# Chunked attention followed by a gated feed-forward layer: crossbar transposes, block-diagonal attention matmuls, and per-token division

## The chip, the cores and the metric

The kernel runs on 1 core of one Trainium2 chip. The metric is device time in microseconds (us), the median over repeated executions. The profile's span is a little shorter than that time: one profiled run of 405.57 us has a span of 403.8 us.

A core has a matmul engine (PE), a vector engine (DVE), an activation engine (ACT), a general engine (POOL) and SP, which in these kernels does nothing but issue DMAs. In this kernel each engine gets one list of instructions and works through it in order.

## The reference

```python
# q, k, v: [batch 8, heads 8, seq 576, dim 64]; chunks of 64 tokens, no attention across chunks
scores = q_c @ k_c.transpose(...) / 8          # 64 x 64 per (batch, head, chunk)
attn   = exp(scores - max); attn /= attn.sum(-1) + 1e-9
out    = attn @ v_c
x      = out as [4608 tokens, 512]
h      = x @ w_in                               # 512 -> 2048
g      = h * (1 / (1 + exp(-beta * h)))
return g @ w_out                                # 2048 -> 512, float32
```

Both kernels work in 9 blocks of 512 tokens, with bfloat16 matmuls. The two dense layers, mm1 (`x @ w_in`) and mm2 (`g @ w_out`), take 1,152 matmuls of 128x512. Four of them start every 0.864 us in the trace, so they need 1152 / 4 x 0.864 = 248.8 us at full clock, or 27.65 us per block. Everything above that is what a rewrite can win.

## The kernel before

A small scheduler collects calls with `at(time, function, ...)`, sorts them by that made-up time (16 units to a block in this kernel), and so fixes the order of every engine's list. Times are only an order. The parts that matter, with cuts marked `...`:

```python
def transpose_dma(blk):                 # q and k of a block, 32 tiles of 128x128, one DMA
    P.dma("sp", lambda e: e.dma_start_transpose(qkT[...], qkcast[...]), ...)

def scores(blk, hp):                    # 64 matmuls of 64x64x64 per block
    ...
    e.matmul(A[64*g:64*g+64, ...], kT[r, 2*cc+g, :], qT[r, 2*cc+g, :])

def sums(blk, bank):                    # softmax denominators: 16 matmuls against a matrix of ones
def invert(blk, bank):                  # DVE: reciprocal, Rhi, Rs
def spread(blk, u, banks):              # 16 matmuls carry the reciprocals to all the rows
    ...
    e.matmul(A[:, banks[g], col:col+128], sel[:, u, ...], Rs[:, :])
def normalize(blk, u, g, bank):         # DVE: o * reciprocal, written straight into xT
    ...

def mm2(blk, s, part, bank):
    ...
    if part == 3:                       # result copied by ACT, stored by ACT's own DMA queue
        P.dma("act", lambda e: e.dma_start(out[n0:n0+128, :], ostage[...]), ...)

for blk in range(3, NB):
    ...
    loads = 30.5 if blk == 3 else t0 - 24
    for which in range(2):
        at(loads, load_qk, blk, which)
    at(loads + 0.1, load_v, blk)
    ...
    at(41 if blk == 3 else t0 - 15.5, transpose_dma, blk)
    attention(blk, t0, u)
```

SP carries loads and one transpose per block. The attention result x is produced already transposed by the matmuls, and the stores are on ACT's queue.

The softmax here doesn't subtract the row's maximum and nothing guards it: scores larger than these inputs give would overflow.

## Time and profile before

| | before |
|---|---|
| time, median of 3 runs | 345.63 us (344.17 to 346.78) |
| span of the profile | 342.4 us |
| needed by mm1 and mm2 at full clock | 248.8 us |
| period of a steady block (start of scores to start of scores) | 32.6 us |
| first mm1 | 24.5 us |

From the page of the kernel before, parts 1, 2 and 4 (busy time of each engine; the span in 40 slices, busy share in tenths; the engines' shares of the chain of work that ended last, where SPq is SP's queue):

```profile
PE 298.1 (87%) x2645; PEld 147.6 (43%) x2688; DVE 150.3 (44%) x234; ACT 167.6 (49%) x264; POOL 112.6 (33%) x124
PE   1559978886598969989998999999999999999996
PEclk9999999999879989999999999999999999999999
DMA  7988997988999889889982990450000000110012
PE 69%; ACT 7%; DVE 7%; DMA 7%; SPq 5%; issue 3%; POOL 1%; ACTq 0%; POOLq 0%
```

PE is the bound: it is busy nearly everywhere after the start, and 69% of the last chain is PE.

From the timeline of PE in the kernel before (start us, duration us, engine, line, operation, output and inputs, shapes, number; in brackets the idle time just before and what ended it): one scores group, one AV group (the attention weights times v), and most of one spread.

```profile
137.45 1.51 PE L383 MATMUL A<-qkO 64*64 64x64 bf16 x64
145.04 0.48 PE L430 MATMUL A<-E,v_bf 64*64 64x64 bf16 x32
130.05 0.56 PE L417 MATMUL A<-Rs,sel 128*128 128x128 bf16 x7 [0.47 <-DVE xT L442]
```

From the timeline of SP in the kernel before, one whole steady period. A duration on SP is the time SP spends issuing, not the transfer.

```profile
185.43 5.72 SPq L341 DMA_TRANSPOSE qkT<-qkcast  x1
191.20 1.24 SPq L268 DMA_DIRECT2D qkstage<-in_q_dram  x2
192.48 1.25 SPq L268 DMA_DIRECT2D qkstage<-in_k_dram  x2
193.77 8.43 SPq L280 DMA_DIRECT2D vstage<-in_v_dram  x4
218.02 5.85 SPq L341 DMA_TRANSPOSE qkT<-qkcast  x1
```

SP works for 16.6 us of the 32.6 and is then free for 16 us.

### The profile page before, as it was taken

How to read it: one execution, taken by the hardware profiler on the slowest of the kernel's cores; microseconds unless marked ns; L12 is line 12 of the kernel's file. 1: busy time of each engine (PE TensorE's matmuls, PEld its weight loads, DVE VectorE, ACT ScalarE, POOL GpSimd, SP SyncE). 2: the span in 40 equal slices, each digit the busy share in tenths (PEclk: the TensorE clock that was granted, in tenths of full speed). 3: DMA queues.
4: the chain of work that ended last, by engine and by line, in shares of the span. 5: the costliest groups of instructions: out<-in, count | busy, mean ns of one | idle time of the engine just before them, and what ended most of it. 6: DMA issues, size and time to landing. Idle time of an engine off the chain costs nothing.

```text
span 342.4 us, 6271 instructions
## 1 busy us (share of the span) xinstructions
PE 298.1 (87%) x2645; PEld 147.6 (43%) x2688; DVE 150.3 (44%) x234; ACT 167.6 (49%) x264; POOL 112.6 (33%) x124
## 2 busy tenths in 40 slices
PE   1559978886598969989998999999999999999996
PEld 0433335443334434534454454445444444444442
DVE  3354712484443455255534543463356336443300
ACT  1545725476234625464455546554655565544421
POOL 0366602334187582690096019403800000000000
PEclk9999999999879989999999999999999999999999
DMA  7988997988999889889982990450000000110012
GB/s 244 292 325 305 300 237 203 222 233 189 188 221 184 211 182 218 227 227 207 240 181 49 267 270 33 93 93 33 31 33 31 33 33 31 47 48 31 31 65 90
DMA packets 79116, 52.85 MB, mean 154 GB/s; under 512 B 65776, under 2 KB 65776, under 8 KB 79088
## 3 DMA queue, kind: packets, MB, share of 16 engines
q1 hardware_dynamic: 71840, 43.00, 52.2%
q10 hardware_dynamic: 7248, 9.45, 8.2%
q8 instruction: 21, 0.34, 0.4%
q14 instruction: 7, 0.06, 0.0%
HBM read 36.71 MB, written 9.44 MB: 135 GB/s over the span
## 4 chain that ended last, share of the span: by engine, by line
PE 69%; ACT 7%; DVE 7%; DMA 7%; SPq 5%; issue 3%; POOL 1%; ACTq 0%; POOLq 0%
PE F L469 30%; PE F L453 30%; DMA qkstage<-in_k_dram 5%; ACT tt L459 3%; SPq L268 3%; PE A L383 3%; PE A L417 3%; DVE R L403 2%; DVE g L462 2%; PE A L430 2%; SPq L341 2%; DMA qkstage<-in_q_dram 2%; DVE Rs L407 1%; ACT E L390 1%; PE A L396 1%
## 5 line engine op out<-in xcount | busy, mean ns | idle before, releaser
L462 DVE SCALAR_TENSOR_TENSOR g<-tt,F 128x512 bf16<-128x512 bf16 x144 | 99.0, 687 | 145.5 <-ACT tt L459 145.4
L459 ACT ACTIVATE tt<-F,beta_half 128x512 bf16<-128x512 f32 x144 | 98.9, 687 | 117.2 <-PE F L453 117.1
L453 PE MATMUL F<-xT,w_in_bf 128*128 128x512 bf16 x549 | 146.0, 391 | 4.3 <-issue 1.8
L469 PE MATMUL F<-w_out_bf,g 128*128 128x512 bf16 x560 | 140.8, 379 | 2.2 <-issue 1.1
L453 PEld LDWEIGHTS F<-xT,w_in_bf 128*128 128x128 bf16 x576 | 55.5, 100 | 68.4 <-issue 6.1
L469 PEld LDWEIGHTS F<-w_out_bf,g 128*128 128x128 bf16 x576 | 54.9, 98 | 64.6 <-DVE g L462 1.1
L330 POOL COPY qkO<-qkT 128x1024 bf16<-128x1024 bf16 x24 | 45.9, 1954 | 75.0 <-PE A L383 55.0
L330 POOL CAST qkcast<-qkstage 128x1024 bf16<-128x1024 f32 x28 | 28.2, 1041 | 23.6 <-DMA qkstage<-in_k_dram 9.9
L474 ACT ACTIVATE ostage<-F 128x512 f32<-128x512 f32 x36 | 21.5, 597 | 25.7 <-PE F L469 25.7
L330 POOL CAST v_bf<-vstage 128x512 bf16<-128x512 f32 x36 | 21.0, 615 | 23.9 <-DMA vstage<-in_v_dram 23.9
L442 DVE TENSOR_TENSOR xT<-o_sb,A 128x512 bf16<-128x512 f32 x36 | 24.1, 681 | 3.3 <-ACT o_sb L437 2.2
L417 PE MATMUL A<-Rs,sel 128*128 128x128 bf16 x144 | 12.9, 239 | 14.5 <-DVE Rs L407 10.9
L437 ACT ACTIVATE o_sb<-A 128x512 f32<-128x512 f32 x32 | 18.8, 593 | 10.3 <-ACT ostage L474 4.6
L390 ACT ACTIVATE E<-A 128x512 bf16<-128x512 f32 x36 | 20.7, 594 | 5.9 <-PE A L383 3.8
L417 PEld LDWEIGHTS A<-Rs,sel 128*128 128x128 bf16 x144 | 10.0, 107 | 21.0 <-DVE Rs L407 15.0
L383 PE MATMUL A<-qkO 64*64 64x64 bf16 x576 | 12.7, 196 | 4.7 <-DVE qkO L330 2.8
L383 PEld LDWEIGHTS A<-qkO 64*64 64x64 bf16 x576 | 11.5, 110 | 8.3 <-issue 3.6
L403 DVE RECIPROCAL R<-A 128x128 f32<-128x128 f32 x9 | 8.6, 952 | 11.3 <-PE F L430 6.1
L357 PE MATMUL F<-identity,qkcast 128*128 128x128 bf16 x32 | 4.1, 311 | 9.3 <-DVE qkcast L330 7.9
L322 POOL CAST w_out_bf<-wstage 128x512 bf16<-128x512 f32 x16 | 9.1, 613 | 5.5 <-DMA wstage<-in_moe_w_out_dram 5.5
L310 POOL CAST w_in_bf<-wstage 128x512 bf16<-128x512 f32 x14 | 8.3, 630 | 5.4 <-DMA wstage<-in_moe_w_in_dram 5.2
L430 PEld LDWEIGHTS A<-E,v_bf 64*64 64x64 bf16 x512 | 5.8, 111 | 7.4 <-issue 3.6
(32 smaller groups left out, 66.5 us busy)
## 6 DMA issues: line engine op xcount, KB each, us to landing
out_dram<-ostage ACTq DMA_DIRECT2D x36, 256.0 KB, 2.6
vstage<-in_v_dram SPq DMA_DIRECT2D x32, 256.0 KB, 8.8
wstage<-in_moe_w_in_dram SPq DMA_DIRECT2D x4, 1024.0 KB, 9.8
wstage<-in_moe_w_out_dram SPq DMA_DIRECT2D x4, 1024.0 KB, 9.6
qkstage<-in_q_dram SPq DMA_DIRECT2D x4, 512.0 KB, 4.1
qkstage<-in_k_dram SPq DMA_DIRECT2D x4, 512.0 KB
qkstage<-in_q_dram SPq DMA_DIRECT2D x4, 448.0 KB
qkstage<-in_k_dram SPq DMA_DIRECT2D x4, 448.0 KB
```

The costliest lines, as they stand in the source:

```text
L330: P.op(eng, lambda e: e.tensor_copy(dst, src), reads, writes)
L383: return e.matmul(A[64 * g:64 * g + 64, 2 * u + hb, col:col + 64], kT[r, 2 * cc + g, :], qT[r, 2 * cc + g, :])
L390: P.op("act", lambda e: e.activation(E[:, bank, :], A[:, bank, :], AF.Exp, scale=0.125), reads=[K("A", bank, v=("s", blk))], writes=[K("E" ...
L403: P.op("dve", lambda e: e.reciprocal(R[:, :], A[:, bank, 0:128]), reads=[K("A", bank, v=("l", blk))], writes=[K("R", v=blk)])
L417: return e.matmul(A[:, banks[g], col:col + 128], sel[:, u, 2 * (2 * w + ch) + g, :], Rs[:, :])
L437: P.op("act", lambda e: e.activation(o_sb[:, g, :], ps[:, bank, :], AF.Copy), reads=[K(psname, bank, v=("o", blk, u))], writes=[K("o_sb", ...
L442: P.op("dve", lambda e: e.tensor_tensor(xT[:, sx, 2 * u:2 * u + 2, :].rearrange("p w (c g i) -> p w c g i", c=4, g=2)[:, :, :, g, :], o_sb ...
L453: P.op("pe", lambda e, c=c: e.matmul(F[:, bank, :], w_in_bf[:, c, 128 * t:128 * t + 128], xT[:, sx, c, :], start=(c == 0), stop=(c == NC - ...
L459: P.op("act", lambda e: e.activation(tt[:, T % 3, :], F[:, bank, :], AF.Tanh, scale=beta_half[:, t:t + 1]), reads=[K("F", bank, v=("h", T) ...
L462: P.op("dve", lambda e: e.scalar_tensor_tensor(g2[:, sg, t, :], tt[:, T % 3, :], 1.0, F[:, bank, :], ALU.add, ALU.mult), reads=[K("F", ban ...
L469: P.op("pe", lambda e, t=t: e.matmul(F[:, bank, :], g2[:, sg, t, 128 * s:128 * s + 128], w_out_bf[:, t, :], start=(t == 0), stop=(t == NT ...
L474: P.op("act", lambda e: e.activation(ostage[:, N % NOS, :], F[:, bank, :], AF.Copy, scale=0.5), reads=[K("F", bank, v=("o", N))], writes=[ ...
```

## The change

The intent is to take attention work off PE. Scores and AV become full 128-row matmuls: k is widened into block-diagonal 128x128 tiles (two heads at once), so a block needs 32 score matmuls instead of 64. v gets a column of ones, so AV yields the softmax denominator as its 65th column. Then `sums` and `spread` disappear, and DVE divides per token. The price is that x now comes out with tokens on rows and must be transposed, which is given to the DMA crossbar. The first two blocks are worked by halves so that mm1 can begin sooner. The diff, 931 lines, cut to its core:

```diff
+        def scores(h, u, n, tiled=False):            # h is half a block: 256 tokens
+            ...
+                kk = kO[...] if tiled else kBD[:, s, hp, c, :]
+                e.matmul(..., kk, q_of(h, r, c, hp))  # q: every 4th element of qkT
+        def attend(h, u, banks, tiled=False):
+            ...
+                e.matmul(unit_out(banks[hp2], c, 65, r), EBD[:, s, u, i, :],
+                         v_bf[r, sv, 2 * u + hp2, 4 * hv + c, 0:65])
-        def sums(...) / invert(...) / spread(...)
+        def normalize(h, u, banks):
+            P.op("dve", lambda e: e.reciprocal(R[:, u, :, :], o[:, :, :, 64]), ...)
+            P.op("dve", lambda e: e.tensor_tensor(xn[...], o[:, :, :, 0:64], R[...], ALU.mult), ...)
+        def turn_x_dma(h):                           # 16 tiles of 128x128, twice per block
+            P.dma("sp", lambda e: e.dma_start_transpose(xT[...], xn[...]), ...)
-            P.dma("act", ... out[n0:n0 + 128, :] ...)
+        def store(blk, s, n, cols=(0, 512), eng="act", queues=("sp", "sp")):
+            ...                                      # two DMAs of 64 rows
+        def load_qk(h, which, queue):
+            ...                # last block, which gathers from 8 batches: 4 DMAs for each of the others' one
+        for blk in range(3, NB):
+            b = begin(blk)                           # 90 + 29.5 * (blk - 3)
+            for h in (2 * blk, 2 * blk + 1):
+                for which in range(2):
+                    at(b - 34, load_qk, h, which, "sp")
+            for hb in range(2):
+                at(b - 33.5, load_v, blk, hb, (0, 1), "sp")
+            rest(2 * blk, b - 27, b - 24.5, b - 20.5, b - 15, 1.74, b - 9.5, b - 17)
+            rest(2 * blk + 1, b - 24, b - 21.5, b - 15.5, b - 10, 1.74, b - 4.5, b - 12)
```

`rest(h, tc, tx, tk, t0, step, tX, tv)` places the cast of q and k at `tc`, their transpose at `tx`, the widening of k at `tk`, scores to division from `t0` on, the transpose of x at `tX` and the cast of v at `tv`.

## The prediction

> **What bounds it now.** TensorE. The page's part 1 has PE 87% busy; the expert layer alone is 1,152 matmuls of 128x512, and in the timeline four of them start every 0.864 us, so they need 248.8 us at full clock. Span 342.4 us: 94 us are lost to them:
> 1. Start. The first mm1 begins at 24.5 us (timeline).
> 2. Until about 105 us. The busy windows show some 235 of the 1,152 matmuls done by then, so about 54 us were lost (start included). The chain of waits gives: loads of k to 84.0, cast, DMA transpose (5.60 us to issue), loads to 104.0, reordering on POOL (1.95 us each).
> 3. Steady blocks. The reciprocal recurs every 32.6 us (185.6, 218.2, 250.8), against 27.65 us for 128 matmuls: 4.9 us of attention per block. Timeline: 64 scores matmuls 1.44 us, AV 2x0.5, sums 0.4, spread 2x0.5, the rest drains around tiled forms and waits for Rs, xT.
>
> **What the change does to PE.** Sums and spread go (the ones column gives the sum, DVE divides per token). Scores become 32 and AV 32 matmuls per block, 128 stationary columns and 64/65 moving. The spread matmuls (128x128, new weights each) run at 57 ns; half the columns should cost 28 to 57. I take 35 ns, 2.2 us per block (estimate; the Trainium skill, "TensorE: Matmul & The Clock Gate", Back-to-back issue gap, puts the floor near 25 ns). No tiling switch remains in steady blocks. Steady block: 32.6 to about 30 us, 6 times, saving 16 us.
>
> **Early part.** The first half block needs half the q, k, v, and no reciprocal, Rhi, Rs, spread chain. First mm1 near 17 to 18 us, not 24.5. Block 1 by halves fills the gap 41 to 75. Loads run in the windows at 385 GB/s for weights and q/k, about 225 for v (256-byte rows). Weights (21.5 us), four blocks of q, k, v (41 us), block 2's transposes and stores (13 us): block 3's q and k are in near 70 us, against 104 now. Lost PE time to the steady state: about 25 us instead of 54.
>
> **Other engines, off PE's path.** Per block: POOL about 15 us, ACT 18, DVE 15. DMA is tight: transposes go from 32 tiles of 128x128 per block to 48. The six now take about 7.5 us of all 16 engines each (busy windows 218 to 226), for 1 MB that loads in 2.7. The Trainium skill ("Advanced Engine Details and Errata", X-Bar Transpose) has transposes as fast as regular DMAs; this trace doesn't agree. Estimate per block: q, k 5.5, v 4.7, transposes 11.2, store 3: 24.4 of 30 us. SP issues all of it, near 25 us per block, stores behind loads.
>
> **Sum.** 248.8 + 25 (start and early) + 7 x 2.2 + 3 (tail) + 3 (median over span) = 295 us. Range 284 to 308. Chances: faster by over 2% 0.97, same 0.02, slower 0.01.
>
> **What shows it.** Busy windows: first mm1 by 18 us; period of the scores 29.5 to 30.5 us, POOL, ACT, DVE below 65%. Timeline: 16 score or AV matmuls in 0.4 to 0.9 us with no idle before them. PEclk 1.0 after 20 us; DMA over 80% busy until the last loads.
>
> **What would make it wrong.** SP or the DMA engines saturate: PE idles before scores or mm1 for a transpose (300 to 315 us). Strided q reads slow matmuls. If nothing waits: 284.

## The result, and the profile after

| | before | after |
|---|---|---|
| time, median of 4 runs | 344.9 us (343.31 to 346.78) | 403.38 us (399.67 to 405.57) |
| ratio of fast runs | 1 | 1.1695, 95% interval 1.1611 to 1.1779 |
| mean granted PE clock | 0.985 | 0.915 |

A ratio here is the mean time of one kernel's fast runs over the mean of the other's of the same rounds, so it is not quite the ratio of the medians quoted beside it. Executions over 1.5% slower than the fastest of the same kernel are left out of the means. The change is 17% slower; the prediction was 15% faster.

The page of the kernel after, the same parts as shown of before:

```profile
PE 308.0 (76%) x2020; PEld 158.9 (39%) x2049; DVE 145.0 (36%) x257; ACT 168.8 (42%) x275; POOL 130.4 (32%) x191
PE   1688986895698896898489938993899305899996
PEclk9999998898889998999699968998899855999999
DMA  9997997992822695179516970699053295130112
PE 47%; SPq 18%; DMA 13%; DVE 7%; POOL 5%; ACT 5%; issue 4%; POOLq 0%; ACTq 0%
```

No engine got much more work. What changed is the shape. PE now has a hole in every block, with the clock dropping after it, and DMA comes in bursts with holes between. SP's queue went from 5% to 18% of the last chain, DMA from 7% to 13%. An on-and-off rhythm in two engines that are both far from full is what a loop of dependencies looks like.

To find the loop, follow one period. From the timeline of SP in the kernel after, with cuts marked:

```profile
213.63 1.23 SPq L445 DMA_TRANSPOSE xT<-xn  x1
214.91 1.26 SPq L259 DMA_DIRECT2D qkstage<-in_q_dram  x2
...
218.78 1.25 SPq L259 DMA_DIRECT2D qkstage<-in_k_dram  x2
220.08 8.14 SPq L281 DMA_DIRECT2D vstage<-in_v_dram  x8
228.26 1.39 SPq L510 DMA_DIRECT2D out_dram<-ostage  x2
229.70 3.70 SPq L347 DMA_TRANSPOSE qkT<-qkb  x1
...
256.57 1.23 SPq L445 DMA_TRANSPOSE xT<-xn  x1
```

From the timelines of POOL and of PE in the same period:

```profile
235.51 4.66 POOL L215 COPY kBD<-qkT 64x256 bf16<-64x256 bf16 x8 [8.31 <-DMA qkT<-qkb]
238.50 0.39 PE L381 MATMUL A<-qkT,kBD 128*128 128x64 bf16 x4 [6.87 <-POOL kBD L215]
248.32 0.43 PE L414 MATMUL A<-v_bf,EBD 128*128 128x65 bf16 x8 [1.48 <-DVE xn L429]
259.76 1.02 PE L460 MATMUL F<-xT,w_in_bf 128*128 128x512 bf16 x4 [0.93 <-DMA xT<-xn]
```

Read together: at 213.63 SP gets to issue the x transpose of one block. Only then can it issue the loads of the next block, which stand behind it, and only after the loads the transpose of q and k, at 229.70. POOL can start widening k at 235.51, PE starts the scores at 238.50 after idling 6.87 us, and division and x transpose of that block follow at 256.57, where the circle starts again. It took 42.9 us:

| step of the circle | us |
|---|---|
| SP issues x transpose, 8 DMAs of q and k, 8 of v, 2 of stores (213.63 to 229.70) | 16.1 |
| transpose of q and k, issue to POOL's start (229.70 to 235.51) | 5.8 |
| widening until the first scores (235.51 to 238.50) | 3.0 |
| scores, exp, AV, division of both halves, with the mm1 and mm2 matmuls that stand between them in PE's list, until x transpose (238.50 to 256.57) | 18.1 |

From the waits of SP's queue in the kernel after (waiting instruction, what released it: us in total, times, longest):

```profile
SPq L445 <- DVE xn L429: 60.4, 6, 12.2
SPq L510 <- ACT ostage L209: 41.8, 11, 9.3
```

SP stands still for 60.4 us in front of x transposes, waiting for the division. In the kernel before there is no such wait, because SP carried nothing that waits for the attention result. That is theory A: **the order in SP's queue closes a loop**. These rivals also fit a slower kernel with more DMA work:

- B: DMA throughput. The transposes are dear (the prediction feared this), so the engines are saturated.
- C: the sum of SP's issue time.
- D: the strided read of q, or POOL's and DVE's extra work.

The busy windows speak against B, C and D already. Columns: window, length, busy us (instructions) of PE, PEld, DVE, ACT and POOL, granted PE clock, DMA share, GB/s. First before, in the four us that hold most of its q and k transpose; then after, in one period:

```profile
220.00:222.00 2.00, 1.95 (x45) 1.08 (x44) 0.57 (x1) 0.69 (x1) 0.00 (x0) 1.00 1.13 262
222.00:224.00 2.00, 2.00 (x11) 0.92 (x10) 1.29 (x2) 0.49 (x1) 0.00 (x0) 1.00 1.62 212
```

```profile
196.00:238.00 42.00, 32.19 (x188) 15.45 (x192) 14.32 (x24) 17.65 (x28) 15.44 (x23) 0.91 0.67 137
```

The share is packet time over the time of 16 engines, and the lines of before show that it can go over 1 while transposes run, so the times of packets overlap. The transposes are dear, as the prediction had it, but the average of a steady period is only 0.67, and no engine but PE passes 18 of 42 us. SP's issues from 213.63 to 256.57 add up to 28 of 42.9 us. These readings are arguments, not proofs, so experiments were made. They hold for the steady part alone: in the kernel after the DMA share is 1.01 from 0 to 20 us and 0.95 from 20 to 60 us (busy windows), so B isn't excluded for the start.

### The profile page after: what moved, and what is told of

Read it like the earlier page. It is cut to its first block, busy times and chain, and to the rows that moved or that the text cites. A ratio compares the mean times of both kernels' runs of the same rounds, so it can differ in the third digit from the quotient of the medians.

```text
span 403.8 us, 5337 instructions
## 1 busy us (share of the span) xinstructions
PE 308.0 (76%) x2020; PEld 158.9 (39%) x2049; DVE 145.0 (36%) x257; ACT 168.8 (42%) x275; POOL 130.4 (32%) x191
## 4 chain that ended last, share of the span: by engine, by line
PE 47%; SPq 18%; DMA 13%; DVE 7%; POOL 5%; ACT 5%; issue 4%; POOLq 0%; ACTq 0%
PE F L491 20%; PE F L460 17%; DMA qkT<-qkb 8%; SPq L281 7%; SPq L267 5%; POOL kBD L215 5%; SPq L259 4%; DVE g L478 4%; PE A L381 3%; ACT tt L475 3%; PE A L414 3%; DMA xT<-xn 3%; PE A L460 2%; DVE xn L429 2%; SPq L510 2%
## 5 line engine op out<-in xcount | busy, mean ns | idle before, releaser
L478 DVE SCALAR_TENSOR_TENSOR g<-tt,F 128x512 bf16<-128x512 bf16 (+1 forms) x148 | 92.3, 629 | 201.5 <-ACT tt L475 201.2
L460 PE MATMUL F<-xT,w_in_bf 128*128 128x512 bf16 (+1 forms) x608 | 142.2, 368 | 14.7 <-DMA xT<-xn 7.7
L491 PE MATMUL F<-w_out_bf,g 128*128 128x512 bf16 (+1 forms) x563 | 146.8, 390 | 2.9 <-issue 0.8
L475 ACT ACTIVATE tt<-F,beta_half 128x512 bf16<-128x512 f32 (+1 forms) x148 | 93.5, 641 | 117.7 <-PE F L460 116.6
L215 POOL COPY kBD<-qkT 64x256 bf16<-64x256 bf16 x112 | 64.7, 619 | 64.2 <-DMA qkT<-qkb 63.0
L215 POOL CAST qkb<-qkstage 128x1024 bf16<-128x1024 f32 x32 | 33.1, 1039 | 125.0 <-DMA qkstage<-in_q_dram 86.6
L381 PE MATMUL A<-qkT,kBD 128*128 128x64 bf16 x224 | 18.7, 235 | 49.5 <-POOL kBD L215 49.5
L398 ACT ACTIVATE EBD<-A 64x512 bf16<-64x512 f32 x56 | 32.9, 587 | 55.9 <-PE A L381 55.2
L209 ACT ACTIVATE ostage<-F 128x512 f32<-128x512 f32 (+1 forms) x36 | 21.3, 591 | 26.6 <-PE F L491 20.6
L429 DVE TENSOR_TENSOR xn<-A,R 128x512 bf16<-128x512 f32 x36 | 24.9, 691 | 1.2
```

The costliest lines, as they stand in the source:

```text
L209: P.op("act", lambda e: e.activation(dst, src, AF.Copy, **kw), reads, writes)
L215: P.op(eng, lambda e: e.tensor_copy(dst, src), reads, writes, rows)
L381: return e.matmul(unit_out(n, i, 64, r).rearrange("k (i t) -> k i t", i=8), kk, q_of(h, r, c, hp))
L398: P.op("act", lambda e, r=r: e.activation(EBD[r, s, u, :, r.start:r.stop], bank(n)[r, :].rearrange("p (x q) -> p x q", q=64), AF.Exp, scal ...
L429: P.op("dve", lambda e: e.tensor_tensor(xn[:, s, :, u, :].rearrange("p c (b d) -> p b c d", b=2), o[:, :, :, 0:64], R[:, u, :, :].unsqueez ...
L460: return e.matmul(bank(n)[:, 64 * c0:64 * c1].rearrange("p (c t) -> p c t", t=64), w_in_bf[:, kt, 128 * t:128 * t + 128], xT[:, sx, c0:c1, ...
```

## The experiments

All edits are to the kernel after. Each group of runs shared one chip and the runs of the kernel before; "ratio" is to before. "Period" is from the start of one block's scores to the start of the next block's; the periods named last are of the last block. Every run's output agreed with the reference within the comparison's tolerance. The times expected by theory A were mostly missed, e1 to e7 and e9_sp all on the slow side; e10 and e11 met theirs. What tells the theories apart is therefore the periods and the traces, more than the totals.

### First group: what is the loop made of?

**e1: the loads of blocks 4 to 8 stand half a block earlier.** The same DMAs and bytes; only their place in SP's list moves, ahead of the x transposes.

```diff
-                    at(b - 34, load_qk, h, which, "sp")
+                    at(b - (50 if blk > 3 else 34), load_qk, h, which, "sp")
-                at(b - 33.5, load_v, blk, hb, (0, 1), "sp")
+                at(b - (49.5 if blk > 3 else 33.5), load_v, blk, hb, (0, 1), "sp")
```

> One change of order: from block 4 on, q, k and v are issued on SP before the previous block's x transposes, not behind them. Same bytes, same instructions. Theory A (a loop through the in-order SP queue: x transpose waits for the division, the next loads wait behind it, then q/k transpose, widening, scores, AV, division): the 14.8 us between the last x transpose and the q/k transpose leave the loop, the period of the scores falls from 42.9 us to 30 to 33 us, time about 347 us (340 to 362). Theory B (the DMA engines are short of throughput because of 1.5 times the transposes): nothing moves, 395 to 405 us. Theory C (SP's own issue time in sum is the bound): nothing moves either.

Measured: 371.72 us, ratio 1.0761 (1.0681 to 1.0842). The first four periods from block 3 on fell from 38.3, 41.2, 42.0 and 42.7 to 33.5, 33.5, 33.2 and 37.2. In the steady part the loop no longer sets the period. The gain of 32 us was smaller than the 56 us put down for it, and the time lies outside the expected 340 to 362; the trace shows why. The busy window of one period of e1:

```profile
185.00:218.00 33.00, 30.38 (x189) 15.12 (x191) 14.11 (x24) 17.30 (x29) 15.15 (x22) 1.00 0.81 173
```

The same work in 33 us: DMA share 0.81 instead of 0.67, clock 1.00 instead of 0.91. So the DMA engines could do more all along (against B), and the lower clock of the kernel after was a consequence of PE's waits, not a cause. SP issues in the new order, x transposes first, then q and k, then the next loads (timeline of SP in e1):

```profile
200.50 1.23 SPq L445 DMA_TRANSPOSE xT<-xn  x1
203.41 1.24 SPq L510 DMA_DIRECT2D out_dram<-ostage  x2
204.70 3.14 SPq L347 DMA_TRANSPOSE qkT<-qkb  x1
```

Much of the rest of the loss is in the last two periods (37.2 and 51.2). The last block's q and k come from 8 batches in 32 small DMAs, which now stand in front of the x transposes of block 7, and PE waited (timeline of PE in e1):

```profile
290.11 1.86 PE L460 MATMUL F<-xT,w_in_bf 128*128 128x512 bf16 x4 [16.87 <-DMA xT<-xn]
```

**e2: only the loads of v move, to behind the transposes of q and k.** This takes 8 us of issue out of the circle's first row.

```diff
-                at(b - 33.5, load_v, blk, hb, (0, 1), "sp")
+                at(b - (21.4 if blk > 3 else 33.5), load_v, blk, hb, (0, 1), "sp")
```

> Only v moves: from block 4 on its loads are issued after both q/k transposes of their block. q and k stay behind the x transposes. Theory A: 8.1 us of v issue leave the loop in 5 blocks, 40 us less, about 363 us (355 to 375), period about 35 us. Theory B and C: same bytes and same issues, 395 to 405 us.

Measured: 400.75 us, ratio 1.1602 (1.1518 to 1.1686), almost nothing; after a first period of 33.5 they are again 39.1 to 41.0 us. That was a miss: the edit moved the last wait instead of removing it. v itself became the thing that came last (timeline of PE in e2):

```profile
240.61 0.60 PE L414 MATMUL A<-v_bf,EBD 128*128 128x65 bf16 x8 [5.88 <-POOL v_bf L215]
```

SP still issues the same list between two x transposes. In the circle before the scores of 231.05, the step from the x transpose to the first transpose of q and k fell from 16.1 to 8.4 us, but from these scores to the next x transpose it took 22.95 us instead of 18.1, so most of the gain was lost again.

**e3: the stores go to ACT's queue, as in the kernel before.**

```diff
-        def store(blk, s, n, cols=(0, 512), eng="act", queues=("sp", "sp")):
+        def store(blk, s, n, cols=(0, 512), eng="act", queues=("act", "act")):
```

> Only the output stores move, from SP's queue to ACT's, as in the kernel before. Theory A: stores take 2.6 us of each loop and one early stall of 4.7 us, so 403 falls to 383 to 396 us; the loads still wait behind the x transposes and the period stays above 39 us. If the stores' waits (SP waits 41.8 us for ostage) were the main cause, the time would fall below 370 us. Theory B: same.

Measured: 415.54 us, the median of four executions of which one (419.82) was slow; the three fast ones have a median of 413.67, and the ratio of fast runs is 1.2024 (1.1929 to 1.2119). That is slower by 10 us, against the expectation. Block 3's scores did come earlier, at 112.2 instead of 116.9 us, but the steady periods rose to 45.1 to 46.1. The circle's steps show where. From the first load to the first transpose of q and k SP needs 13.6 us instead of 14.8. From the issue of that transpose to POOL's start it takes 8.8 us (229.60 to 238.37) instead of 5.8. The other steps changed by less than 0.3 us. The two transposes of q and k now follow each other directly, with 8.68 us of issue for the pair, where the kernel after spends 3.70 and 3.69 with a store between. Why the first then lands later isn't shown. ACT also spends 1.26 us to issue two stores in a list that holds the gate of mm1; what that costs wasn't measured alone.

**e4: x is transposed on PE, not by a DMA.** This takes the waiting instruction out of SP's list.

```diff
-            at(tX, turn_x_dma, h)
+            for u in range(2):
+                at(tX + 0.8 * u, turn_x_pe, h, u, (A2, A3)[u], ("act", "dve")[u])
```

> All x transposes on PE, as in the first two blocks: SP has no instruction left that waits for the division. Theory A: SP runs ahead, loads are limited by the stage buffers alone, period 31 to 34 us, 340 to 360 us, although PE gets 16 transposes of 128x128 more per block (about 1 us). Theory B: a third of the transposed tiles is gone, 370 to 385 us. With the first run this tells order from traffic: if both are near 350, order is enough.

Measured: 386.52 us, ratio 1.1199 (1.1138 to 1.126), periods 36.0 to 38.2 us and, last, 52.0. By its total this run is nearer to what was expected of B (370 to 385) than of A (340 to 360); that DMA traffic is not the reason is read from e1, which kept all the traffic. The gain is half of e1's, because another waiting instruction took the place of the first. From the timeline of SP in e4, four stores of mm2 results, the later ones waiting for theirs (the line's 15.62 us include the wait), with the next loads behind them:

```profile
225.18 15.62 SPq L510 DMA_DIRECT2D out_dram<-ostage  x4
240.84 1.26 SPq L259 DMA_DIRECT2D qkstage<-in_q_dram  x2
```

This reads as e1 does: what matters is what stands in front of the loads, not how much SP issues. No run moved these stores alone on top of e4.

### Second group: the last block, both repairs at once, and the strided q

In the kernel after, the last block took 56.2 us instead of 42. The timelines of SP and PE there:

```profile
299.88 5.68 SPq L267 DMA_DIRECT2D qkstage<-in_q_dram  x8
...
316.81 5.56 SPq L267 DMA_DIRECT2D qkstage<-in_k_dram  x8
```

```profile
337.38 0.39 PE L381 MATMUL A<-qkT,kBD 128*128 128x64 bf16 x4 [20.77 <-POOL kBD L215]
338.58 1.48 PE L491 MATMUL F<-w_out_bf,g 128*128 128x512 bf16 x3 [0.22 <-issue]
339.86 1.91 PE L460 MATMUL F<-xT,w_in_bf 128*128 128x512 bf16 x4
341.57 0.65 PE L381 MATMUL A<-qkT,kBD 128*128 128x64 bf16 x8
```

32 DMAs of 64 KB cost SP 22.4 us, 0.70 us each, no less than the 0.62 us of a load of 256 KB in the other blocks; PE idled 20.77 us. After it, four mm1 matmuls took 341.57 - 339.86 = 1.71 us instead of 0.864, and the granted clock from 338.6 to 341.6 us was 0.50. That is half speed, as the Trainium skill ("TensorE: Matmul & The Clock Gate", Part 1: The HAM clock gate) says of an array that has been idle. So a wait costs more than its own length.

**e5: e1, and the last block's 32 DMAs are spread in groups of 4 over the two blocks before.**

```diff
+                        for hb in range(2):
+                            at(b - (76 if h % 2 == 0 else 54) + 5 * (2 * which + hb),
+                               load_qk, h, which, "sp", (hb,))     # last block only
```

> The early loads of e1, and the 32 separate q and k loads of the last block (its rows lie in eight places, 0.70 us of SP each, 22.4 us in one go) are issued four at a time over the two blocks before. The same issues in the same sum. Order theory: the 16.9 us wait for x before the last block and most of the 37.2 and 51.2 us periods go, periods near 33.4 us throughout, 118 + 5 x 33.4 + 64 = 349 us (345 to 358). Theory C (the sum of SP's issue time is the bound): moved, not removed, 365 us or more.

Measured: 364.98 us, ratio 1.056 (1.0506 to 1.0614). The last period fell from 51.2 (e1) to 36.9, but the one before it rose from 37.2 to 43.4, with SP issuing almost without a gap from 216 to 248 us and PE waiting for an x transpose in that crowd (timeline of PE in e5):

```profile
245.54 1.86 PE L460 MATMUL F<-xT,w_in_bf 128*128 128x512 bf16 x4 [9.37 <-DMA xT<-xn]
```

The time misses the order theory's 345 to 358 us and is at the 365 put down for theory C. Here C is true for one block: where 16 more DMAs were put in, SP's issues cover 41.6 of the 43.4 us.

**e6: e1 and e4 together.**

```diff
-                    at(b - 34, load_qk, h, which, "sp")
+                    at(b - (50 if blk > 3 else 34), load_qk, h, which, "sp")   # v likewise
-            at(tX, turn_x_dma, h)
+            for u in range(2):
+                at(tX + 0.8 * u, turn_x_pe, h, u, (A2, A3)[u], ("act", "dve")[u])
```

> The early loads of e1 and all x transposes on PE; the last block's loads stay in one go. SP then waits for no division. If the x transposes' place in SP's order is what e1 still pays: the 16.9 us stall becomes small, since the last block's loads only delay q/k transposes that are due later; periods 33 to 34 us (PE has 1 us more), 355 to 362 us. If it is the DMA traffic of the x transposes, the periods themselves fall below 32 us.

Measured: 367.94 us, ratio 1.0643 (1.0582 to 1.0703), outside the expected 355 to 362. Its steady periods of 35.6 to 36.0 are longer than e1's 33.4: the transposes and their waits for the division (1.89 and 0.36 us in one block) are now on PE. The last block gains, 39.5 instead of 51.2.

**e7: e6, the last loads spread as in e5, and the second AV group and the x transposes placed 0.8 to 0.9 units later, so that the division is done when PE arrives.**

```diff
-                at(t0 + step * (u + 1.5), attend, h, u, (A2, A3))
+                at(t0 + step * (u + 1.5) + 0.9 * u, attend, h, u, (A2, A3))
-                at(tX + 0.8 * u, turn_x_pe, h, u, (A2, A3)[u], ("act", "dve")[u])
+                at(tX + 0.8 + 0.9 * u, turn_x_pe, h, u, (A2, A3)[u], ("act", "dve")[u])
```

> e5 and e6 together, and the second AV of each half block 0.9 us later in the order so that PE has a matmul group to do while DVE divides (that wait is 1.48 us a block). Order theory: periods near 32 us, 117 + 5 x 32 + 64 = 341 us (336 to 350), about the kernel before. DMA theory: e6 already has this.

Measured: 356.85 us, ratio 1.0321 (1.0269 to 1.0372), outside the expected 336 to 350; periods 35.8, three times 34.8 and, last, 38.2.

**e8: q is read densely from the transposed tile.** The 64 elements are the wrong ones: it measures the read alone. The wrong result still passed the comparison; the reference draws q and k with a scale of 0.1, so the scores lie near zero.

```diff
-                "k i (c t h) -> k c h i t", c=4, h=4)[:, chunk, hp, :, :]
+                "k (c x) (h i t) -> k c x h i t", c=4, h=2, i=8)[:, chunk, hp % 2, hp // 2, :, :]
```

> Wrong result on purpose: the changed kernel, but the scores matmuls read q as 64 adjacent elements in place of every fourth. If the stride is why eight scores take 0.45 us where eight AV take 0.26 us, they take about 0.26 us (32 ns each); time falls by at most 1 us, as the loop stays. If it is the block-diagonal weights (their loading) or the output pattern, they stay at 0.45 us (56 ns each).

Measured once: 397.85 us, state unknown. From the chain of work of the kernel after, and of e8 (start us, us, what):

```profile
206.68 0.46 PE A L381 x8
```

```profile
204.14 0.23 PE A L381 x8
```

A scores matmul takes 58 ns with q at every fourth element and 29 ns with q dense. So theory D is real in kind, but 32 x 29 ns = 0.9 us per block is the whole of it, against a period of 42; e8's periods stayed at 41.

### Third and fourth group: the start, and a version that beats both

**e9: from the kernel after, with four output buffers, the last block's q and k staged in the buffer the weights no longer need, its 32 loads spread over the whole steady part, q and k early as in e1, v a block earlier, attention 1.5 units earlier, each second AV 0.9 units later, and the early order of e10 below.** Once with those 32 loads on SP (e9_sp), once on ACT's queue (e9_act). If the sum of SP's issues counted, ACT should win.

```diff
-                                qkstage[32 * c:32 * c + 32, s, which, hb, :],
+                                wstage[32 * c:32 * c + 32, 2 * hv + which, 512 * hb:512 * hb + 512],
+                            at(73 + 15 * (4 * (h % 2) + 2 * which + hb), load_qk, h, which, "sp", (hb,))
```

> A version by the order theory, all on SP's queue: q and k loads right after the q/k transposes of the block before; v one place earlier still; x transposes stay on DMA; the last block's 32 q and k loads go into the weights' staging buffer (free by then) and are issued four at a time over 120 us; block 2's second q/k transpose before block 3's loads; four output buffers, not three; each second AV 0.9 us later. Order theory: scores of block 3 near 107 us (117 in the changed kernel), periods near 31.5 us, 107 + 5 x 31.5 + 64 = 329 us (322 to 340), faster than both. If SP's issue time in sum (about 30 us a block) binds: periods 33 us or more, 338 us or more.

> As e9_sp, but the last block's 32 loads are issued by ACT. If SP's sum of issue time binds in e9_sp, this one is faster by 3 us or more; if SP has room, it is slower by 0 to 6 us, because each issue holds ACT for about 0.65 us before a tanh, as the stores did in e3.

Measured: 352.34 us, ratio 1.0228 (1.0159 to 1.0298), and 353.86 us, ratio 1.0254 (1.0173 to 1.0335). There is no clear difference between them: taking 22 us of issue off SP gained nothing. That speaks against the sum of SP's issues as the bound of e9_sp, but doesn't settle it, since ACT now pays for these issues and could hide a gain. Both miss the order theory's 322 to 340 us, and e9_sp's periods of 34.0 to 37.4 lie in the range (33 us or more) that was put down for the sum of issues. Both ratios are above 1, but by 2% or more is unclear. Early on PE waits for x of block 2, whose transpose again stands behind loads (timeline of PE in e9_sp):

```profile
106.49 1.86 PE L465 MATMUL F<-xT,w_in_bf 128*128 128x512 bf16 x4 [10.51 <-DMA xT<-xn]
```

**e10: the kernel after with only the early part repaired: four output buffers, block 2's transposes of q and k before other work, v of block 2 later.** In the kernel after, the second of those transposes was issued at 88.75 us although its data were ready, behind the loads of block 3 (timeline of SP):

```profile
79.98 8.67 SPq L281 DMA_DIRECT2D vstage<-in_v_dram  x8
88.75 2.87 SPq L347 DMA_TRANSPOSE qkT<-qkb  x1
```

```diff
-        NOS = 3
+        NOS = 4
-        rest(4, 53, 55.2, 58.5, 62.5, 0.8, 66, 61)
-        rest(5, 55, 57.3, 61.5, 65, 0.8, 68.5, 64)
+        rest(4, 48.6, 49.8, 58.5, 62.5, 0.8, 66, 61)
+        rest(5, 54, 55.9, 61.5, 65, 0.8, 68.5, 64)
-            at(46, load_v, 2, hb, (0, 1), "sp")
+            at(50, load_v, 2, hb, (0, 1), "sp")
```

> The changed kernel with the first part alone mended: block 2's q/k transposes ahead of v 2 and of block 3's loads in SP's order, and four output buffers. Order theory: the 4.7 us wait of PE for an output buffer and the 3.2 us wait for the widened k go, scores of block 3 start near 107 us; the loop of the later blocks stays at 42 us, so the time is 403 less 8 to 12 us, about 393 us. If the early loss is DMA throughput, scores of block 3 stay at 115 to 117 us.

Measured: 394.1 us, ratio 1.1434 (1.1348 to 1.152). The scores of block 3 start at 108.8 instead of 116.9 us, and the end comes 9 us sooner, as expected: what is lost early stays lost, and the loop behind it runs on (steady periods up to 42.4, last period 56.7).

**e11: everything together, x of block 2 on PE, and for the later blocks an order of SP by need: the q and k transposes of the next block stand next to the x transposes of this one, the loads behind both and a block ahead of their use.**

```diff
-                rest(2 * blk, b - 28, b - 25.5, ...)          # e9
+                rest(2 * blk, b - 42, b - 37.5, b - 30, b - 16.5, 1.74, b - 10.5, b - 25)
+                rest(2 * blk + 1, b - 38, b - 34.8, b - 26, b - 11.5, 1.74, b - 5.5, b - 23)
```

> e9_sp reordered where its profile still shows SP's order: both q/k transposes of the next block stand next to the x transposes of this one (in e9 they stood behind v, stores and the last block's loads, 15 us after their casts had ended), and block 2's x is turned on PE (in e9 its transpose stood behind block 3's q/k transposes and PE waited 10.5 us). Order theory: scores of block 3 at 100 to 106 us, waits of PE for the widened k gone, periods 31 to 32.5 us, 104 + 5 x 32 + 64 = 328 us (322 to 338), 3 to 6% below the kernel before. If SP's sum of issue time binds, periods stay at 34 to 35 us and the time at 342 to 350 us.

Measured: 336.15 us (332.92 to 337.49), ratio 0.9737 (0.9648 to 0.9825) against 345.09 us: faster than both kernels. The whole interval is below 1, though it doesn't clear 2% throughout. Timeline of SP in e11, and the busy window of one period:

```profile
150.15 3.11 SPq L352 DMA_TRANSPOSE qkT<-qkb  x1
153.30 1.32 SPq L450 DMA_TRANSPOSE xT<-xn  x1
154.66 2.07 SPq L352 DMA_TRANSPOSE qkT<-qkb  x1
156.78 6.09 SPq L282 DMA_DIRECT2D vstage<-in_v_dram  x8
```

```profile
170.00:202.00 32.00, 30.36 (x190) 14.82 (x188) 13.87 (x24) 17.62 (x28) 15.60 (x22) 1.00 0.84 194
```

The period from block 3 to block 4 is 37.3, those after it are 32.7 to 33.4 us, and the DMA engines move 194 GB/s at a share of 0.84, against 137 GB/s and 0.67 in the kernel after. The arithmetic and the transposes are still those of the change, apart from block 2's x. SP's issues now cover 31.0 of the 32.65 us from 169.76 to 202.41, a larger share than in the kernel after (28.1 of 42.9). So the sum wasn't what held the kernel after, but in e11 there is little left before it would bind.

### What PE lost, and where

Count the mm1 and mm2 matmuls that the timeline shows by a given moment (half-width ones as half; the count scaled up to 1,152 because the trace misses a few per cent), multiply by 0.216 us, and subtract from the clock. That is the time PE lost until then, in us:

| until (us) | before | after | e11 |
|---|---|---|---|
| 60 | 36.3 | 31.4 | 29.6 |
| 100 | 56.6 | 53.7 | 45.7 |
| 120 | 59.8 | 62.5 | 51.5 |
| 200 | 76.3 | 87.7 | 65.4 |
| 280 | 89.0 | 113.4 | 79.2 |

From 100 to 280 us before loses 32.4 us and e11 33.5: in the steady part the new attention, even well ordered, is no better than the old one. e11 wins what it wins in the first 100 us, 10.9 us.

## Why the prediction was wrong

The prediction said 295 us (284 to 308); it measured 403. The miss of 108 us can be laid out by the starts of the scores: block 3 at 116.9, block 7 at 281.2, block 8 at 337.4, end of the span 66.4 later.

1. **"SP issues all of it, near 25 us per block, stores behind loads": the step that failed.** The size was about right (28 us of issue per period). What was wrong was to hold a sum against a period of 30 us and conclude that it fits. The queue is in order, one of its entries waits for the division, and the next block's loads stand behind it. Four periods took 281.2 - 116.9 = 164.3 us instead of 120, that is 44 us. e1 showed it by moving the loads alone, which brought three of the periods to 33.2 to 33.5 us. The prediction did list "PE idles before scores or mm1 for a transpose" among the ways to be wrong, but put it down to SP or the DMA engines saturating and limited it to 315 us. Neither saturated in a steady period of the kernel after (SP issued for 28 of 42.9 us, DMA share 0.67).
2. **The last block was not costed at all.** Its period was 56.2 us instead of 30, 26 us more. Some 12 of these are the loop again; the other 14 come with the 32 separate loads, 22.4 us of issue. The diff shows them, in `load_qk`. e5 showed that taking them out of that place shortens the last period by 14 us, at the price of the block where they were put.
3. **"Lost PE time to the steady state: about 25 us instead of 54."** Until the scores of block 3 at 116.9 us it was about 62, some 37 more. The first mm1 came at 20.8 us, not at 17 to 18, which is 3 of it. The order of SP's early work, with its loads and stores in front of transposes, is 8 us by e10 (a fourth output buffer included, whose share isn't separated), and 11 by e11's lost time at 120 us (51.5 against 62.5). The rest wasn't taken apart. DMA throughput is an open rival here: the share is 0.95 to 1.01 in the first 60 us of the kernel after, and 1.09 to 1.11 from 60 to 117 us in e11. Besides, in e11 PE is busy for 17.0 of the 20 us from 60 to 80, while the lost time still grows by 9.1. Half-block attention and its transposes occupy PE there without advancing mm1 and mm2.
4. These three make about 107 of the 108 us. The end after block 8's scores, 66.4 us, was not costed separately and can hide a few us.
5. **"I take 35 ns, 2.2 us per block ... about 30 us."** Mechanism right, size off. Eight scores took 0.46 us and eight AV 0.26 us, so four groups of each take 2.9 us. A steady block with the loop broken has 27.65 + 2.9 = 30.5 us of PE work, and 2.4 us of waits in e1 that the prediction had set to zero (1.48 for the division, because the second AV group uses the banks that DVE still reads, and 0.92 for the x transpose). That gives 33.0 against 33.4 measured. So the 2.6 us per block that the change was to save were not saved in any run: the shortest steady period in any of them is 32.65 us (e11), against 32.6 before.
6. **What held.** Per-block work of POOL, ACT and DVE was predicted as 15, 18 and 15 us and measured as 15.4, 17.7 and 14.3. "Strided q reads slow matmuls" was named as a risk and is true, at 0.9 us per block. "DMA over 80% busy" was wrong for the steady part of the kernel after (0.67) and right once the order was repaired (0.81 to 0.84): it describes the kernel the prediction imagined.

What stays open: why in e3 the transposes of q and k took 3 us longer to land, which part of the early loss in point 3 belongs to which step or to DMA throughput, and how far a shorter way from scores to x transpose on PE (18.1 us of the circle) would have opened the loop; no run changed that alone.

## What to carry to other kernels

When a change puts an instruction that waits for a result into a queue that also feeds the next round, draw the circle: what waits, what stands behind it, and what that has to feed before the wait can end again. The length of the circle, not the sum of the queue's work, is then the period, as long as the queue itself isn't full (as SP was in one block of e5); if the circle is longer than the compute period, move the loads a round ahead of the waiting instruction. Read one full period of the issuing queue's timeline, including its free time, before trusting any engine's busy share, and look for the one block whose loads are shaped differently.

## What the Trainium skill lacked or had wrong

- "DMA: Bandwidth & Descriptors", Issuing engines are not separate DMA queues, calls the sequencer's time to initiate a DMA usually small relative to the DMA itself. Here SP took 0.62 us per load of 256 KB and 0.70 us per load of 64 KB, 22.4 us for 32 of them. The section doesn't say what a wait in the issuing queue does to the DMAs behind it. The skill does place a DMA's semaphore wait on the issuing sequencer, but no page draws the loop that can follow; moving the loads out of it alone brought the period from 42 us to 33 (e1).
- "Perfetto Trace Analysis", What "DMA-bound" means, has a solid sequencer track as the sign of a sequencer bound. SP issued for 28 of 42.9 us and set the pace all the same, by order. A point about in-order loops is missing there.
- "Advanced Engine Details and Errata", X-Bar Transpose (TRN2), has transposes as fast as regular DMAs. In the kernel before, the DMA shares of the four windows of 2 us from 218 to 226 us, in which a transpose of 32 tiles (1 MB) ran beside at most a store or two, are 0.36, 1.13, 1.62 and 0.66: 7.5 us of packet time on 16 engines. SP's issue of it took 5.85 us, and the median from issue to landing of these transposes is 7.2 us. The same 1 MB of plain load takes 2.7 us at the 385 GB/s that the weights reached.
- "SBUF — State Buffer", Specifications, asks for at least two hits per 16-byte line for full bandwidth, with a penalty for each cross to a new line. Two hits were not enough here: the scores' q, every fourth bfloat16 and so two hits per line, took 58 ns per matmul of 64 columns, against 29 ns dense (e8).
- "TensorE: Matmul & The Clock Gate", Back-to-back issue gap, gives about 131 ns per matmul of 512 columns as the sustained rate with a new weight load each, and calls its 216 ns an over-count. Here four such matmuls, each with its own weights, started every 0.864 us, so 216 ns each, the figure that the page measures for back-to-back matmuls in its Part 1. The floor of about 25 ns for up to 64 columns roughly agrees with the 29 ns of e8.
